# A long convolution and a shift mixer on one core: the filter's transposes in halves by parity, its first DFT step on 64-row tiles, and a new order of work

## The chip, the core and the metric

The kernel runs on one core of a Trainium2 chip. A core has five engines that run side by side, each through its own queue in order: TensorE (PE, matrix products, weights loaded by separate instructions that the profile calls PEld), VectorE (DVE), ScalarE (ACT), GpSimd (POOL) and SyncE (SP), which here issues nearly all DMA transfers. Operands lie in SBUF, 128 partitions wide; PE writes into PSUM, and what PE wrote has to be copied out ("evacuated") by ACT or DVE before the PSUM bank can be used again. The metric is the time of one execution on the device in microseconds; lower is better.

## The reference

Two branches over the same 2048 x 640 input are computed and then mixed by a gate.

```python
g = sigmoid((x * gate_w).sum(-1, keepdims=True))
# A: short causal convolution of k (4 taps), times v, then a long convolution by FFT
k_shift = sum over t<4 of k_pad[:, t:t+S, :] * shift_k[:, 3-t]
kv = k_shift * v
y = irfft(rfft(kv padded to 2S) * rfft(ssm_k padded to 2S))[:S] + kv * ssm_D
a = q * y
# B: a mixer that shifts four channel groups along the sequence, then an MLP
h  = gelu(layernorm(x) @ w1)
hs = concat(shift_1(h0), shift_-1(h1), shift_2(h2), shift_-2(h3)) @ w2
x1 = x + hs
b  = x1 + gelu(layernorm(x1) @ w3) @ w4
return g * a + (1 - g) * b
```

S is 2048, the width D is 640, the MLP's inner width 1536; inputs and output are bf16. `ssm_k` is the filter, given as 640 rows of 2048 time steps.

## The kernel before

The 2048 time steps are laid out as 128 partitions times 16 steps. Branch B is a chain of matmuls with 128-row weights: `mlp1` (w1), `w2`, `w3`, `w4`, with a layer norm before the first and the third. Branch A computes the long convolution as a DFT in steps, all on PE:

- `tap` makes kv from k, v and the four taps, by matmuls with diagonal weights on 64-row tiles.
- `step1` is the first DFT step, of length 128, over the partition axis. It is done for kv (name `KV`) and for the filter (name `HT0`) in four pieces `c` of five units each; a unit is two matmuls, `r` = 0 for the even and 1 for the odd rows, into two PSUM banks. Each bank is evacuated by ACT or DVE, as a string of letters A and V in the step's name says, into a staging buffer `stg`, of which there is one for each `c` and `r`. When all five units are in, `send` stores the buffer to a scratch tensor in DRAM (`S_x` for kv, `S_h` for the filter).
- `gather` reads the scratch back in another order (`ax`); `step2` and its products with `CMP` are the second DFT step, on 64 x 32 tiles; `product` multiplies the two spectra on DVE; `step3` (`INV`) starts the way back on 32 x 64 tiles; its result goes through DRAM again (`S_g`, `gin`), and `step4` (`F4`) finishes, with the gate and q.

The filter has time along the free axis, so `h_transpose` first turns it on PE. In each of ten banks PE transposes eight 128 x 128 blocks whose columns lie 16 elements apart; the block is the stationary operand (the weights), the identity the moving one. The result `HT0` has its rows in natural order. kv has even rows in partitions 0 to 63 and odd ones in 64 to 127, so that its two matmuls of a unit each use half of PE's rows and can run side by side. For the filter the split by parity is in the weights instead: `F1N` is a table of its own with zero rows, and both matmuls use all 128 rows.

Tables of sines are made in the kernel (`f1_table`, `f1n_table`, `f4_table`, `t2_table`, `i_tables`): DVE makes the angles, ACT takes the sine. ACT evaluates sine, GELU and tanh from tables that have to be loaded first, when a function of another table comes up.

The order of all this is written out by hand as one long list, `ORDER`. An entry such as `step1.HT0.2.AAAAAVAAAA:12` names a function, its arguments and the step to issue; the list fixes the order of instructions in each engine's queue. Which buffer of a ring an allocation takes is written out too, in `SLOTS`: "c" for the four PSUM banks, "row" for the four large row buffers that the staging buffers `stg`, the loaded k (`kn`), the normalised x (`xn`) and others share in turn, "gt" and so on. An allocation waits until the last user of its slot is done, a store to DRAM included.

Lines that the profile names and that are spoken of below: L227 warm-up matmuls; L369 and L371 evacuations by ACT and DVE; L395 the filter's transposes; L422 the filter's `step1`, L424 kv's; L434 `send`; L441 `gather`; L462 `step2`; L509 `step3`; L560 and L618 the loads and transposes of k (L618 also x's); L590 `tap`; L709 `mlp1`; L720 the gate's matmuls; L786 `w2`; L813 the transposing DMA of the normalised x1; L834 `w3`; L839 its GELU and L856 `w4`.

Of the kernel before, what the change touches and what calls it, by code (L numbers as in the profile page):

```python
# [16 lines left out]
P = 128  # L17
# [24 lines left out]
def kernel(  # L42
# [24 lines left out]
        "c": "012301230213012310323103120132103123010320130213102321032103230120312013201320132031203102313201"  # L67
             "203213021021323013203210312300123120231203123012130120313021323013223102103120310321032013212032"
             "310230121303120301202130321231030122103032101231302031230123210123012031203103220133012301231023"
             "103120312031201023102",  # L70
        "m": "0100100101010101010101010101010101011010101010110101010101011010101",
        "row": "01230121032130301230123102310320230202023",
        "gt": "012301202120103102012301201",
        "xt": "010101",
        "gq": "012201201102102101202102102101102101",
        "ax": "0123023102130213",
# [32 lines left out]
    F1N = const.tile([P, 2, H, 2], BF16, name="F1N")  # L109
# [53 lines left out]
    def col(i):  # L163
        return sm[:, i:i + 1]
# [87 lines left out]
    def bit(k):  # L252
        return BF[:, k:k + 1]
# [32 lines left out]
    def f1n_table():  # L286

        ts(col(27), bit(0), -1.0, pf[:], op1=ALU.add)
        ts(col(28), col(27), 0.5)
        n = tab([P, H, 2], "n")  # L290
        ts(n[:, :, 0], R64[:, 0:H], col(27), col(28))
        ts(n[:, :, 1], n[:, :, 0], float(128 + 128), op0=ALU.add)
        ts(n[:, :, 0], n[:, :, 0], float(64 + 128), op0=ALU.add)
        yield from sin_table(F1N[:, 0], n, 256)
        yield
        V.tensor_scalar(out=F1N[:, 1], in0=F1N[:, 0], scalar1=bit(0), scalar2=None, op0=ALU.mult)
        V.tensor_tensor(out=F1N[:, 0], in0=F1N[:, 0], in1=F1N[:, 1], op=ALU.subtract)

# [85 lines left out]
    def h_transpose(dc, ev):  # L384
# [4 lines left out]
        def make(hh):  # L389
            box = {}  # L390

            def first():
                ps = box["ps"] = slot(psc, [P, 8, P], BF16, "pst", "c", 4)
                for i in range(8):
                    PE.transpose(out=ps[:, i, :], in_=hv[:, 8 * hh + i, :], identity=IDB[:])  # L395

            def second():
                evac(ev[hh], dst[:, 8 * hh:8 * hh + 8, dc * P:(dc + 1) * P], box["ps"][:])
            return first, second
# [9 lines left out]
    def step1(name, c, ev):  # L409
# [5 lines left out]
        def make(u):  # L415
            ps = []

            def first():
                for r in range(2):
                    ps.append(slot(psc, [P, 512], F32, "ps1", "c", 4))  # L420
                    if name == "HT0":
                        PE.matmul(ps[r][:], lhsT=F1N[:, r].rearrange("p a b -> p (a b)"), rhs=src[:, o + 512 * u:o + 512 * u + 512], start=True, stop=True)  # L422
                    else:
                        PE.matmul(ps[r][:], lhsT=F1[HALF[r]].rearrange("p a b -> p (a b)"), rhs=src[HALF[r], o + 512 * u:o + 512 * u + 512], start=True, stop=True,  # L424
                                  tile_position=(H * r, 0))
# [444 lines left out]
    def step4(t1, ev):  # L870
# [238 lines left out]
```

## Time and profile before

| What | us |
|---|---|
| timed runs, median of 3 (lowest, highest) | 242.7 (242.56, 243.21) |
| the profiled execution | 241.72 |
| its span, first to last instruction | 239.9 |
| PE, DVE, ACT, POOL busy in it | 227.0, 191.6, 176.6, 17.6 |

The profile lists groups of instructions by source line and engine: how often, busy time, mean duration in ns, and then the idle time of the engine just before them with what ended it. A duration is an instruction's own length, and instructions of PE overlap: a matmul of 512 columns is shown with some 380 ns although the next one starts 215 ns later, so PE's pace is read from start to next start. A timeline row gives start, length from the first start to the last end, engine, line, operation, output and input, their shapes, and how many were merged. A row of stretches gives for each engine its busy time and, in brackets, its instruction count, then the granted clock of PE as a share, the DMA engines' share and GB/s.

### The profile page before, as it was taken

To read this page: it belongs to the slowest core of one execution; us is meant where nothing else is said; L and a number is where in the kernel's file an instruction comes from. 1 tells how busy PE (TensorE), PEld (TensorE's weight loads), DVE (VectorE), ACT (ScalarE), POOL (GpSimd) and SP (SyncE) were. 2 spreads that over 40 slices of the span, in tenths; PEclk is the share of its full clock that TensorE was granted. 3 is DMA by queue.
4 is the path that set the end of the run, shared out by engine and by line. 5 is a ranking of instruction groups with operands and counts; after the bars stand their busy time and mean duration, and the time that the engine had idled before them with its cause. 6 is when DMAs were issued, how large, how long until landed. Compare 5 with 4: busy or idle time off the path is not lost.

```text
span 239.9 us, 5658 instructions
## 1 busy us (share of the span) xinstructions
PE 227.0 (95%) x2260; PEld 115.2 (48%) x2260; DVE 191.6 (80%) x454; ACT 176.6 (74%) x318; POOL 17.6 (7%) x34
## 2 busy tenths in 40 slices
PE   6799999999999978889999999999999999999993
PEld 2477575434665534334355344454444455436651
DVE  6999999889889973768769796869768996408994
ACT  4599999779999939998956778848478353636660
POOL 3243220000002000040000300000000000000000
PEclk9999999999999999999999999999999999999998
DMA  6999386793997994998699791089970026599644
GB/s 248 397 369 330 123 188 111 253 351 128 356 401 234 331 271 140 277 380 329 194 304 323 191 245 70 0 158 368 354 221 0 20 93 221 196 378 398 231 164 167
DMA packets 42887, 57.06 MB, mean 238 GB/s; under 512 B 20329, under 2 KB 35690, under 8 KB 42606
## 3 DMA queue, kind: packets, MB, share of 16 engines
q1 hardware_dynamic: 42286, 54.10, 69.7%
q0 software_dynamic: 576, 2.62, 3.1%
q8 instruction: 17, 0.28, 0.5%
q14 instruction: 8, 0.07, 0.1%
HBM read 34.42 MB, written 18.36 MB: 220 GB/s over the span
## 4 chain that ended last, share of the span: by engine, by line
PE 71%; DMA 14%; ACT 8%; DVE 3%; issue 2%; POOL 1%; SPq 0%; ACTq 0%
PE ps L856 18%; PE ps L834 14%; PE psm L709 9%; DMA S_h<-stg 6%; PE psw L786 6%; PE psk L590 4%; PE ps L884 4%; PE ps L462 3%; PE pst L618 3%; PE ps L509 3%; ACT stg L369 3%; DMA ax<-S_h 3%; PE pst L395 2%; PE ps L422 2%; DMA gin<-S_g 2%
## 5 line engine op out<-in xcount | busy, mean ns | idle before, releaser
L856 PE MATMUL ps<-W,gt 128*128 128x512 bf16 (+1 forms) x384 | 56.8, 300 | 0.3 <-ACT gt L839 0.3
L834 PE MATMUL ps<-x1t,W 128*128 128x512 bf16 x240 | 55.6, 380 | 1.0 <-ACT gt L839 1.0
L856 PEld LDWEIGHTS <-gt 128*128 128x128 bf16 x384 | 29.0, 98 | 25.6 <-issue 4.8
L834 PEld LDWEIGHTS <-W 128*128 128x128 bf16 x240 | 21.9, 98 | 30.0 <-issue 6.0
L369 ACT CAST stg<-ps 128x512 bf16<-128x512 f32 x56 | 29.8, 595 | 6.1 <-DMA S_h<-stg 3.8
L369 ACT CAST gs<-ps 128x320 bf16<-128x320 f32 x44 | 16.2, 440 | 18.8 <-PE ps L509 13.6
L839 ACT ACTIVATE gt<-ps 128x1024 bf16<-128x1024 f32 x24 | 24.8, 1041 | 4.1 <-PE ps L834 4.1
L709 PE MATMUL psm<-xt,WA 128*128 128x512 bf16 x100 | 23.6, 380 | 0.0
L371 DVE CAST stg<-ps 128x512 bf16<-128x512 f32 x24 | 15.9, 686 | 7.4 <-PE ps L422 3.6
L786 PE MATMUL psw<-WA,HT 128*128 128x512 bf16 (+1 forms) x116 | 21.7, 299 | 0.0
L369 ACT CAST hs<-ps 128x512 bf16<-128x512 f32 x25 | 13.5, 593 | 8.2 <-PE ps L462 8.2
L371 DVE CAST XS<-ps 128x512 bf16<-128x512 f32 x22 | 14.6, 685 | 4.4 <-PE ps L462 4.4
L888 ACT ACTIVATE y<-ps,GS 128x320 bf16<-128x320 f32 x25 | 12.3, 527 | 7.8 <-PE ps L884 6.1
L786 PEld LDWEIGHTS <-HT 128*128 128x128 bf16 x116 | 10.0, 98 | 11.5 <-issue 2.5
L371 DVE CAST gs<-ps 128x320 bf16<-128x320 f32 x20 | 9.0, 485 | 7.8 <-PE ps L509 5.8
L788 DVE SCALAR_TENSOR_TENSOR X<-psw,X 128x640 bf16<-128x640 f32 x16 | 13.1, 817 | 1.9 <-PE psw L786 1.9
L863 DVE SCALAR_TENSOR_TENSOR X<-ps,OMG,X 128x640 bf16<-128x640 f32 x15 | 13.2, 877 | 1.7 <-PE ps L856 1.7
L709 PEld LDWEIGHTS <-WA 128*128 128x128 bf16 x100 | 9.0, 98 | 11.0 <-issue 1.7
L422 PE MATMUL ps<-HT,F1N 128*128 128x512 bf16 x40 | 11.4, 379 | 2.7 <-ACT stg L369 2.5
L371 DVE CAST hs<-ps 128x512 bf16<-128x512 f32 x15 | 9.9, 685 | 4.1 <-PE ps L462 4.0
L462 PE MATMUL ps<-ax,CMP 64*32 64x384 bf16 (+3 forms) x512 | 13.0, 300 | 0.2 <-DMA ax<-S_h 0.2
L712 ACT ACTIVATE HT<-psm 128x1024 bf16<-128x1024 f32 (+1 forms) x12 | 10.6, 895 | 2.4 <-PE psm L709 2.3
(152 smaller groups left out, 356.2 us busy)
## 6 DMA issues: line engine op xcount, KB each, us to landing
S_x<-stg SPq DMA_DIRECT2D x8, 640.0 KB, 3.0
S_h<-stg SPq DMA_DIRECT2D x8, 640.0 KB, 5.6
ax<-S_x SPq DMA_DIRECT2D x8, 640.0 KB, 5.5
ax<-S_h SPq DMA_DIRECT2D x8, 640.0 KB, 5.9
S_g<-gs SPq DMA_DIRECT2D x8, 640.0 KB, 5.4
W<-in_B_w_dram SPq DMA_DIRECT2D x2, 1920.0 KB, 14.0
kn<-in_A_k_dram SPq DMA_DIRECT2D x4, 640.0 KB, 10.2
q<-in_A_q_dram SPq DMA_DIRECT2D x4, 640.0 KB, 5.7
```

The lines of the kernel that those rows point to most:

```text
L369: A.copy(out=dst, in_=src)
L371: V.tensor_copy(out=dst, in_=src)
L422: PE.matmul(ps[r][:], lhsT=F1N[:, r].rearrange("p a b -> p (a b)"), rhs=src[:, o + 512 * u:o + 512 * u + 512], start=True, stop=True)
L462: PE.matmul(ps[j][q:q + 32, lo - 512 * u:hi - 512 * u], lhsT=CMP[HALF[j], 8 * b + 4 * h + i, c, :], rhs=st[name, 2 * b + h][HALF[j], i, lo ...
L709: PE.matmul(ps[:, v, :].rearrange("p (a b) -> p a b", a=4), lhsT=W1N[:, k, 160 * f:160 * f + P] if f < 4 else W1M[:, k, :], rhs=xt[:, :, k ...
L786: PE.matmul(ps[:, o:o + w], lhsT=h_tile(f, t1), rhs=W2P[:, f, o:o + w], start=(f == 0), stop=(f == 4))
L788: V.scalar_tensor_tensor(out=X1[:, t1, :], in0=ps[:], scalar=1.0, in1=X[:, t1, :], op0=ALU.mult, op1=ALU.add, accum_out=S12[:, 0, t1:t1 + 1])
L834: PE.matmul(ps[:, u, :].rearrange("p (a b) -> p a b", a=4), lhsT=st["W3"][:, k, f * P:(f + 1) * P], rhs=xt[:, :, k, :], start=(k == 0), st ...
L839: A.activation(out=gt[:, 2 * (fp % 2):2 * (fp % 2) + 2, :], in_=ps[:], func=ACT.Gelu_apprx_tanh)
L856: PE.matmul(to[:, 0:w], lhsT=st["gt", c, f // 4][:, f % 4, i * P:(i + 1) * P], rhs=st["W4"][:, f, o:o + w], start=(f == 0), stop=(f == FC ...
L863: V.scalar_tensor_tensor(out=X1[:, t1, :], in0=ps[:], scalar=OMG[:, t1:t1 + 1], in1=X1[:, t1, :], op0=ALU.mult, op1=ALU.add)
L888: A.activation(out=box["y"][:], in_=box["ps"][:], func=ACT.Copy, scale=GS[:, t1:t1 + 1])
```

## The change

Three things change in the code, and with them the order.

`h_transpose` turns each block in two halves: the even columns of the block (one in two, so 32 elements apart in memory) go to PE's column tile 0 and partitions 0 to 63, the odd ones to column tile 64 and partitions 64 to 127. There are 160 transposes of 64 columns for 80 of 128, and `HT0` now has kv's parity order. `step1` for the filter then has the same form as for kv: weights `F1` on half the rows, two 64-row tiles. The table `F1N` and its function are gone. The evacuations, their count and their shapes stay.

`ORDER` and `SLOTS` are written anew. The entries are the same but for the three of `f1n_table`; the letters that give an evacuation to ACT or DVE and the places differ. The diff, cut to the code and to those places of the order that the prediction speaks of:

```diff
-    F1N = const.tile([P, 2, H, 2], BF16, name="F1N")
...
-    def f1n_table():
-
-        ts(col(27), bit(0), -1.0, pf[:], op1=ALU.add)
-        ts(col(28), col(27), 0.5)
-        n = tab([P, H, 2], "n")
-        ts(n[:, :, 0], R64[:, 0:H], col(27), col(28))
-        ts(n[:, :, 1], n[:, :, 0], float(128 + 128), op0=ALU.add)
-        ts(n[:, :, 0], n[:, :, 0], float(64 + 128), op0=ALU.add)
-        yield from sin_table(F1N[:, 0], n, 256)
-        yield
-        V.tensor_scalar(out=F1N[:, 1], in0=F1N[:, 0], scalar1=bit(0), scalar2=None, op0=ALU.mult)
-        V.tensor_tensor(out=F1N[:, 0], in0=F1N[:, 0], in1=F1N[:, 1], op=ALU.subtract)
...
                 for i in range(8):
-                    PE.transpose(out=ps[:, i, :], in_=hv[:, 8 * hh + i, :], identity=IDB[:])
+                    for r in range(2):
+                        PE.transpose(out=ps[HALF[r], i, :], in_=hv[:, 8 * hh + i, r:P:2], identity=IDB[:], tile_position=(0, H * r))
...
-                    if name == "HT0":
-                        PE.matmul(ps[r][:], lhsT=F1N[:, r].rearrange("p a b -> p (a b)"), rhs=src[:, o + 512 * u:o + 512 * u + 512], start=True, stop=True)
-                    else:
-                        PE.matmul(ps[r][:], lhsT=F1[HALF[r]].rearrange("p a b -> p (a b)"), rhs=src[HALF[r], o + 512 * u:o + 512 * u + 512], start=True, stop=True,
-                                  tile_position=(H * r, 0))
+                    PE.matmul(ps[r][:], lhsT=F1[HALF[r]].rearrange("p a b -> p (a b)"), rhs=src[HALF[r], o + 512 * u:o + 512 * u + 512], start=True, stop=True,
+                              tile_position=(H * r, 0))
...
-        "open.L1.left:0 open.A2.right:0 load_x0.0:0 consts0:0 consts0:1 warm:0 load_x0.1:0 load_x.1:0 f1_table:0 warm:1 "
-        "pow0:0 x_stats.0.VVVA:0 f1_table:1 warm:2 kv_alloc:0 x_stats.0.VVVA:1 x_stats.0.VVVA:2 x_stats.0.VVVA:3 "
-        "x_stats.0.VVVA:4 x_stats.0.VVVA:5 x_stats.0.VVVA:6 x_norm.0.AVVA:0 f4_table:0 k_load.3.AAA:0 x_norm.0.AVVA:1 "
+        "open.L1.left:0 open.A2.right:0 consts0:0 load_x0.0:0 warm:0 load_x0.1:0 warm:1 consts0:1 f1_table:0 "
+        "k_load.3.AAA:0 x_stats.0.VVVA:0 x_stats.0.VVVA:1 load_x.1:0 x_stats.0.VVVA:2 pow0:0 kv_alloc:0 warm:2 "
+        "k_load.3.AAA:1 x_stats.0.VVVA:3 x_stats.0.VVVA:4 k_load.3.AAA:5 warm:3 load_w1:0 x_stats.0.VVVA:5 f4_table:0 "
+        "f1_table:1 k_load.3.AAA:6 x_stats.0.VVVA:6 x_norm.0.VVAV:0 warm:4 x_norm.0.VVAV:1 x_norm.0.VVAV:2 "
+        "x_norm.0.VVAV:3 k_load.1.VVA:0 x_stats.1.VVVV:0 k_load.2.VVV:0 x_turn.0.VAA:0 x_turn.0.VAA:4 load_x.3:0 "
...
-        "step1.HT0.1.AVAAVAAVAA:12 x1_norm.0.VVVV:5 w2.11:0 w2.5:1 step1.HT0.1.AVAAVAAVAA:13 step1.HT0.3.AVAAAAAAAA:16 "
-        "w2.11:1 step1.HT0.1.AVAAVAAVAA:9 gate:0 step1.HT0.1.AVAAVAAVAA:11 step1.HT0.1.AVAAVAAVAA:14 "
+        "x1_norm.0.AVAV:4 w2.9:1 t2_table:5 step1.HT0.1.VAAAVAAAAV:12 w2.5:0 x1_norm.0.AVAV:5 w2.11:1 "
+        "step1.HT0.1.VAAAVAAAAV:7 gate:0 step1.HT0.1.VAAAVAAAAV:13 step1.HT0.1.VAAAVAAAAV:9 step1.HT0.3.AAAVAAAAAA:16 "
+        "w2.9:2 w2.5:1 i_tables:2 step1.HT0.1.VAAAVAAAAV:10 w2.6:0 step1.HT0.1.VAAAVAAAAV:14 i_tables:3 "
...
+        "step1.HT0.0.VVVVAVVVAA:6 step1.HT0.0.VVVVAVVVAA:11 w3.0.2:1 w3.0.0:0 step1.HT0.0.VVVVAVVVAA:10 "
+        "step1.HT0.0.VVVVAVVVAA:7 step1.HT0.0.VVVVAVVVAA:3 load_w4:0 w3.0.4:0 gate:1 step1.HT0.0.VVVVAVVVAA:8 w2.4:2 "
+        "step2.x.0.VVVAVAAVVV:12 w3.0.0:1 w3.0.4:1 step1.HT0.1.VAAAVAAAAV:15 step1.HT0.0.VVVVAVVVAA:5 "
```

In the third pair of hunks the buffer in question is the odd-row one of piece 3 (`step1.HT0.3...:16` sends it) and its next user the odd-row one of piece 1, first written by `:11` in the old order and by `:14` in the new one.

More of the change, by code (lines that the diff above doesn't have):

```diff
@@ L66 @@
     SLOTS = {
[L67 to L73, printed above, removed]
+        "c": "012320230213230123203120213203102132030210321301230213021032123021031203102310231203301203120310"
+             "312320132031203132021201303210213203102301202132013032101230123013102130231201321302310312020313"
+             "102130213203102312031023210230101320231213020310231213020312130120312030213310201230123012302130"
+             "213012301230213021031",
+        "m": "0101010101010101010101010101010101010101010101010101010101010101010",
+        "row": "01231023012310012301321302310230021302120",
+        "gt": "01230103130121023102301201",
         "xt": "010101",
-        "gq": "012201201102102101202102102101102101",
-        "ax": "0123023102130213",
+        "gq": "012202120121021021012020120121021021",
+        "ax": "0123021302130213",
         "hp": "01231203",
@@ L902 @@
     ORDER = (
[152 rows of a table removed]
[153 rows of a table added]
     ).split()
     calls = dict(warm=warm, pow0=pow0, row_order=row_order, consts0=consts0, load_w1=load_w1, load_gw=load_gw, w1_mixed=w1_mixed, z_rows=z_rows, z_cols=z_cols, load_x=load_x, load_x0=load_x0, x_norm=x_norm, x_turn=x_turn, x_stats=x_stats,
-                 f1_table=f1_table, f1n_table=f1n_table, t2_table=t2_table, i_tables=i_tables, f4_table=f4_table, kv_alloc=kv_alloc, k_load=k_load, k_wrap=k_wrap, v_load=v_load, tap=tap,
+                 f1_table=f1_table, t2_table=t2_table, i_tables=i_tables, f4_table=f4_table, kv_alloc=kv_alloc, k_load=k_load, k_wrap=k_wrap, v_load=v_load, tap=tap,
                  kv_consts=kv_consts, mlp1=mlp1, load_h=load_h, h_transpose=h_transpose,
```

289 rows, old and new, of the table ORDER are left out of this document.

## The prediction

> **What bounds the kernel now.** I read the page's first part, then busy time by stretches, then the chain that ended last, then TensorE's own timeline.
>
> ```profile
> span 239.9 us, 5658 instructions
> PE 227.0 (95%) x2260; PEld 115.2 (48%) x2260; DVE 191.6 (80%) x454; ACT 176.6 (74%) x318; POOL 17.6 (7%) x34
> ...
> 80.00:90.00 10.00, 8.32 (x53) 4.28 (x52) 8.28 (x23) 5.85 (x13) 0.00 (x0) 1.00 1.10 283
> 90.00:100.00 10.00, 8.96 (x48) 4.11 (x47) 6.28 (x14) 9.94 (x22) 0.00 (x0) 1.00 0.64 206
> 100.00:110.00 10.00, 9.04 (x84) 3.76 (x83) 6.51 (x20) 9.81 (x19) 2.43 (x4) 1.00 1.03 348
> 160.00:180.00 20.00, 20.00 (x264) 8.98 (x262) 16.48 (x26) 12.29 (x24) 0.00 (x0) 1.00 0.92 301
> ```
>
> The columns after a stretch's length are the busy times of PE, PEld, DVE, ACT and POOL. PE is busy for 227.0 of 239.9 us and has no gap at all in a stretch such as 160 to 180. Work taken off PE therefore shortens the kernel, unless something else ends last in that place. The one place in mid-kernel where PE is not full is 80 to 110 us: 1.68 + 1.04 + 0.96 = 3.7 us idle, with ACT full from 90 on. That is the stage of the filter's first DFT step.
>
> ```profile
> PE ps L422 <- ACT stg L369: 2.5, 3, 1.7
> ACT stg L369 <- DMA S_h<-stg: 3.8, 1, 3.8
> ...
> 83.29 5.68 DMA S_h<-stg
> ...
> 105.56 9.35 DMA S_h<-stg
> ...
> 115.88 6.01 DMA ax<-S_h
> 121.94 0.63 PE ps L462 x24
> ```
>
> The waits say why. ACT stood 3.8 us for a staging buffer whose store to DRAM was still on its way (the 5.68 us piece of the chain), and PE then stood for ACT, 1.7 us at the longest. After that the chain runs over ACT and two DRAM trips to the first DFT step 2 of the filter at 121.94.
>
> **The change, part by part.**
>
> *Filter's first step (L422).* Forty full-array matmuls become forty on 64 rows, two of which run side by side. The kernel has that form already, in the same step on KV (L424).
>
> ```profile
> 37.67 0.61 PE L424 MATMUL ps<-KV,F 64*128 64x512 bf16 x4
> 38.21 2.33 PE L709 MATMUL psm<-xt,WA 128*128 128x512 bf16 x10
> ...
> 46.60 0.39 PE L424 MATMUL ps<-KV,F 64*128 64x512 bf16 x2
> 46.83 0.38 PE L590 MATMUL psk<-DG,KT 64*128 64x256 bf16 x4
> ...
> 67.61 0.39 PE L424 MATMUL ps<-KV,F 64*128 64x512 bf16 x2
> 67.93 2.22 PE L395 MATMUL pst<-IDB,HN 128*128 128x128 bf16 x32
> ...
> 71.37 1.03 PE L422 MATMUL ps<-HT,F1N 128*128 128x512 bf16 x4
> 72.23 1.03 PE L786 MATMUL psw<-WA,HT 128*128 128x512 bf16 x4
> ```
>
> From start to next start, four L422 matmuls take 0.86 us; four of L424 take 0.54, two of them 0.32. Two take only 0.23 where another 64-row matmul follows (46.60 to 46.83), so leaving that tiling costs about 0.1 us a visit. In the new order PE visits this step twelve times: eight times with four matmuls, four times with two. New cost 8 x 0.54 + 4 x 0.32 = 5.6 us; old 40 x 0.215 = 8.6. **-3.0 us**, the drains included. No bound is far off here, because the same matmul is in the trace.
>
> *Filter's turn (L395).* Eighty transposes of 128 columns become 160 of 64 columns. The two halves of a pair go to column tiles 0 and 64, each with its own weight load, whose elements now stand 64 bytes apart instead of 32.
>
> ```profile
> 59.12 3.19 PE L395 MATMUL pst<-IDB,E 128*128 128x128 bf16 x48
> 62.15 1.03 PE L786 MATMUL psw<-WA,HT 128*128 128x512 bf16 x4
> ...
> L395 PEld LDWEIGHTS <-E 128*128 128x128 bf16 x48 | 3.1, 148 | 0.3 <-issue 0.3
> L618 PEld LDWEIGHTS <-kn 128*128 128x128 bf16 x80 | 4.9, 96 | 0.5
> L509 PEld LDWEIGHTS <-INV 32*64 32x64 bf16 x256 | 3.0, 102 | 6.5 <-issue 5.0 <-DVE p L483 0.4 <-DVE gs L371 0.4
> L720 PEld LDWEIGHTS <-GW 128*1 128x1 bf16 x20 | 0.4, 82 | 0.6 <-issue 0.2
> ...
> 52.11 1.25 PE L720 MATMUL psz<-xt,GW 128*1 128x512 bf16 x20
> 53.30 0.39 PE L424 MATMUL ps<-KV,F 64*128 64x512 bf16 x2
> ```
>
> Now one costs 3.03/48 = 63 ns, 5.05 us for all eighty. A strided load shows 148 ns against 96 for a packed one, so the load sets that pace. No row shows a half turn, so I bound a pair. Column tiles do run side by side: twenty matmuls in four column tiles took 1.19 us, 0.24 for each four of 512 columns. So the low end is 128 columns at that rate, 0.24/4 = 60 ns, or -0.2 us in all. If a load costs by its columns, two halves cost one whole: 63 ns, 0. If it costs by its length (half of what 148 has over the one-column 82, so 115 ns), a half is 63 x 115/148 = 49 ns, a pair 98, **+2.8**. The high end is two whole prices in a row, 126 ns, +5.05. The trace has a hint for the dear side: the 64-column load of INV, 102 ns, is no shorter than the packed 128-column one, 96. I take the middle of the two readings by columns and by length, 80 ns a pair: **+1.4 us** (-0.2 to +5.1). Two more stretches in a tiling of their own, one of them cut in two, add four drains of 0.1, **+0.4**.
>
> The Trainium skill (SBUF — State Buffer, Specifications) has lines of 16 bytes and a penalty for each new line; elements 32 and 64 bytes apart both open a line each, which by itself would leave the price by columns and the term at 0.
>
> *The stall.* In the old order the buffer that ACT waited for is sent four steps before it is taken again, with two Mixer groups of PE between the matmuls that fill it and those that need it; in the new order six steps and three groups. So part of the wait stays: half of the 1.7 us goes, **-0.9** (0 to -3.7, all that idle time). What is late next there is ACT, full from 90 us.
>
> *Evacuations, table loads, tables.* The filter's forty evacuations (HT0) go from 28 on ACT and 12 on DVE to 27 and 13, KV's from 28 and 12 to 25 and 15.
>
> ```profile
> L369 ACT CAST stg<-ps 128x512 bf16<-128x512 f32 x56 | 29.8, 595 | 6.1 <-DMA S_h<-stg 3.8 <-PE ps L424 1.4 <-PE ps L422 0.7
> L371 DVE CAST stg<-ps 128x512 bf16<-128x512 f32 x24 | 15.9, 686 | 7.4 <-PE ps L422 3.6
> L839 ACT ACT_TABLE_LOAD x2 | 2.6, 1283 | 1.6 <-PE ps L834 1.6
> L273 ACT ACTIVATE F1N<-n,NPI 128x128 bf16<-128x128 int32 x1 | 0.5, 455 | 0.0
> L296 DVE TENSOR_SCALAR F1N<-F1N,BF 128x128 bf16<-128x128 bf16 x1 | 0.3, 256 | 0.0
> ...
> 10.00:20.00 10.00, 9.90 (x107) 7.06 (x108) 9.64 (x31) 9.98 (x16) 4.32 (x6) 1.00 1.01 360
> ```
>
> Four casts move, 4 x 0.6 = 2.4 us off ACT and 2.7 onto DVE, which has 3.7 and 3.5 us free in the two stretches from 90 to 110: no cost, and if that cover is gone at most one cast, 0.7. Sine, GELU, sine, GELU, tanh, GELU is the new succession of tables, six loads for seven: 1.28 us less for ACT late, but tanh now falls between two GELUs of the first w3 groups, two loads where PE needs gt. 0 (-1.3 to +1.3). Without F1N's table ACT saves 0.46 and DVE 0.3, a second pass like it and five small operations. Most of that lies between 10 and 20 us, where PE is full: 0 (-0.5).
>
> *Moved steps.* Twelve of the k transposes go ahead of x's first turn, and their load goes ahead of x's second one in SP's queue.
>
> ```profile
> 1.86 6.57 PE L227 MATMUL psz<-WZ 128*128 128x512 bf16 x20 [1.86 <-DVE WZ L223]
> 10.07 0.62 PE L618 MATMUL pst<-IDB,xn 128*128 128x128 bf16 x8 [1.64 <-ACT xn L661]
> ...
> 15.35 2.01 PE L618 MATMUL pst<-IDB,kn 128*128 128x128 bf16 x32
> 17.20 2.32 PE L709 MATMUL psm<-xt,WA 128*128 128x512 bf16 x10
> ...
> 2.13 0.43 SPq L560 DMA_DIRECT2D kn<-in_A_k_dram  x1
> ...
> L813 SPq DMA_TRANSPOSE x1t<-xn x4: 3024/4141/7513, 85.5 to 156.1; - x4
> ```
>
> They cost 12 x 1.85/32 = 0.7 us of PE and fall into its 1.64 us gap before 10.07, if k is there by then; behind them stand only the last warm matmuls and x's turn, which would wait with them. ACT and DVE are as full as PE right after, so **-0.3** (-0.7 to +0.7, if k comes late). The filter's loads, the load of w3 and the stores and gathers change places in SP's queue by an issue or two, 0.4 us each. The last x1t transpose moves behind four gathers and three S_g stores; SP holds 3 to 7.5 us at each such transpose. Its reader, the last quarter of w3, is far off in PE's order, and PE is full there: 0, up to 4.1 us for one median transpose if that cover is gone. The order from DFT step 2 on has the same visits to each tiling (19 of step 2, 14 of step 3): 0.
>
> Sum: -3.0 + 1.4 + 0.4 - 0.9 - 0.3 = -2.4 us. The profiled execution took 241.7 us (span 239.9 and 1.8 around it), which gives 239.3. The three timed runs have a median of 242.7, 1.0 above it, so I predict **240.3** for the median.
>
> **The rivals.**
>
> *The half loads cost whole ones, one after the other.* Place: PE in the two turn stretches at 59 and 68 us, which have no gap to hide in. Price: a pair 126 ns, +5.05 instead of +1.4; with PE later, no stall is won. -3.0 + 5.05 + 0.4 - 0.3 = +2.1: **244.8**. It decides from a pair of 63 + 2.9/80 us = 99 ns on (111 ns if the stall gain comes). For it: INV's half-width load is as long as a full one. Against it: column tiles overlap in L720, if with one-column loads.
>
> The Trainium skill (TensorEngine Tiling (Array Packing), Restrictions and Gotchas) speaks for this rival: column tiling excludes fast weight load. By another page (TensorE: Matmul & The Clock Gate, LDWEIGHTS), columns over 1.2 give 53 ns a half load; two in a row make 107 a pair, by my estimate +3.5 and a sum of +0.6. INV's row agrees with the first rule.
>
> *PE's gain becomes a wait.* The chain into 121.94 is ACT's evacuations, then 9.35 us of S_h store and 6.01 of gather. If the last store still leaves at 105, PE arrives earlier and waits at step 2 (its wait there is now 0.2 us, so there is no slack): all that is won before is lost, and only the -0.3 at the start may stay: **242.4**. For it: ACT full from 90 to 110. Against: the casts that go to DVE.
>
> *The stage runs without gaps.* Turns at the price by columns (0) and all 3.7 us won: -3.0 + 0.4 - 3.7 - 0.3 = -6.6: **236.1**. For it: DVE is a third idle from 90 to 110 and can take ACT's casts. Against: ACT would have to give up more than four.
>
> **How the numbers follow.** Forecast 0.44, dear half loads 0.23, gain waited away 0.16, no gaps 0.17. Changes under 0.3%, 0.7 us, can't be told from none. Faster: 0.43 of the forecast's, 0.17, and 0.03 of the third; same: 0.01, 0.11 and 0.01 of the dear loads; slower: 0.22 of the dear loads and 0.02 of the third, whose lost cover can cost more than the start gives. So 0.63, 0.13, 0.24. The forecast's own range is 238.3 to 242.0 (turns 0 to +2.8, stall -1.7 to 0). With the two outer cases the range is 236.5 to 245.0: it reaches both of them but for the outer half of each.
>
> **What would show it.** L422's matmuls in fours 0.54 us from start to next start; else the first term is wrong. L395's 160 in 6.4 us: near 5 is the price by columns, near 10 the first rival. The ACT wait for S_h<-stg at two to three us instead of 3.8. The first step 2 of the filter at 119 to 120 instead of 121.94; if it is still there with a PE wait for ax<-S_h of 2 us, the second rival is right. A PE wait in front of x's first turn would mean that k came late.

## The result and the profile after

| What | before | after |
|---|---|---|
| median, us (lowest, highest; 4 runs each) | 242.95 (242.56, 243.23) | 239.88 (239.31, 240.34) |
| the profiled execution and its span | 241.72, 239.9 | 240.33, 238.5 |
| PE busy | 227.0 | 228.1 |
| table loads on ACT (`ACT_TABLE_LOAD`) | 7 | 5 |

The changed kernel takes 0.9874 of the old one's time (95% interval 0.9841 to 0.9906): 3.1 us less, and 0.4 us under the forecast of 240.3. PE's busy time *rose* by 1.1 us; what went is waiting. In the new kernel the filter's turn is L382, the first step L408 (for kv and filter alike), `send` L418, `step2` L446, `step3` L493, evacuations L355 (ACT) and L357 (DVE), `w2` L770, `w3` L818, its GELU L823, `w4` L840, the transposes of k and x L602, `tap` L574, the gate's tanh L807.

The stretches of the stage first, with the columns as before (PE, PEld, DVE, ACT, POOL, clock, DMA, GB/s):

```profile
80.00:90.00 10.00, 10.00 (x72) 4.86 (x70) 9.63 (x28) 9.77 (x21) 1.22 (x2) 1.00 0.85 297
90.00:100.00 10.00, 9.41 (x62) 3.88 (x59) 8.80 (x23) 9.13 (x19) 0.00 (x0) 1.00 1.05 299
100.00:110.00 10.00, 9.91 (x91) 4.04 (x88) 7.39 (x16) 9.16 (x18) 1.11 (x2) 1.00 1.06 385
```

In these stretches PE was idle for 3.7 us before; now it is for 0.7, nearly all of it one wait of 0.59 for the transposed x1. ACT's 3.8 us wait for a sent buffer is gone.

PE's timeline round the filter's turn and first step:

```profile
60.19 1.10 PE L382 MATMUL pst<-IDB,E 128*64 128x128 bf16 x16 [0.49 <-ACT stg L355]
61.23 0.39 PE L408 MATMUL ps<-KV,F 64*128 64x512 bf16 x2
61.55 4.68 PE L382 MATMUL pst<-IDB,E 128*64 128x128 bf16 x80
66.16 1.04 PE L770 MATMUL psw<-WA,HT 128*128 128x512 bf16 x4
...
71.95 3.78 PE L382 MATMUL pst<-IDB,HN 128*64 128x128 bf16 x64
75.67 0.18 PE L720 MATMUL psg<-GW,ones 128*128 128x5 bf16 x1
...
77.16 0.61 PE L408 MATMUL ps<-HT,F 64*128 64x512 bf16 x4
77.70 1.04 PE L770 MATMUL psw<-WA,HT 128*128 128x512 bf16 x4
...
83.18 0.39 PE L408 MATMUL ps<-HT,F 64*128 64x512 bf16 x2
83.50 1.04 PE L770 MATMUL psw<-WA,HT 128*128 128x512 bf16 x4
```

Half turns: 1.04 us for 16, 4.61 for 80, 3.72 for 64, so 9.37 for all 160, 58 to 59 ns each, against 5.08 for the eighty whole ones (59.12 to 62.15, 67.93 to 69.98). First step: fours 0.54, twos 0.32.

The start, and the place where the second DFT step of the filter comes in:

```profile
9.01 0.85 PE L602 MATMUL pst<-IDB,kn 128*128 128x128 bf16 x12 [2.46 <-DMA kn<-in_A_k_dram]
...
11.00 1.28 PE L602 MATMUL pst<-IDB,xn 128*128 128x128 bf16 x20
...
26.67 1.94 PE L574 MATMUL psk<-DG,KT 64*128 64x256 bf16 x44
...
121.99 0.63 PE L446 MATMUL ps<-ax,CMP 64*32 64x512 bf16 x24
...
135.93 0.48 PE L493 MATMUL ps<-hs,INV 32*64 32x320 bf16 x16
136.34 2.33 PE L818 MATMUL ps<-x1t,W 128*128 128x512 bf16 x10
```

k came late, x's first turn begins at 11.00 (10.07 before) and the first taps at 26.67 (25.42). The second step is at 121.99, where it was, with no wait ahead of it: until there PE has won back only what it lost before. `step3` now runs in one piece at 135.93; before, two waits of 0.20 for ACT cut it up, so that its next `w3` began at 137.44 in place of 136.34.

ACT at the first GELUs:

```profile
100.61 1.28 ACT L823 ACT_TABLE_LOAD   x1
101.90 1.02 ACT L823 ACTIVATE gt<-ps 128x1024 bf16<-128x1024 f32 x1
102.82 0.58 ACT L355 CAST stg<-ps 128x512 bf16<-128x512 f32 x1
103.29 0.23 ACT L807 ACTIVATE GS<-ZG 128x16 f32<-128x16 f32 x1
...
104.12 1.02 ACT L823 ACTIVATE gt<-ps 128x1024 bf16<-128x1024 f32 x1
```

The tanh at 103.29 stands between two GELUs and loads nothing.

### The profile page after: what moved, and what is told of

It reads as the page before. It is cut to its first block, busy times and chain, and to the rows that moved or that the text cites. A ratio compares the mean times of both kernels' runs of the same rounds, so it can differ in the third digit from the quotient of the medians.

```text
span 238.5 us, 5806 instructions
## 1 busy us (share of the span) xinstructions
PE 228.1 (96%) x2340; PEld 116.6 (49%) x2340; DVE 191.7 (80%) x443; ACT 176.9 (74%) x318; POOL 16.5 (7%) x34
## 4 chain that ended last, share of the span: by engine, by line
PE 80%; DMA 9%; ACT 7%; issue 1%; DVE 1%; SPq 0%; ACTq 0%
PE ps L840 21%; PE ps L818 18%; PE psm L693 9%; PE psw L770 5%; PE ps L446 5%; PE psk L574 4%; PE pst L382 4%; PE ps L868 4%; PE ps L408 3%; DMA kn<-in_A_k_dram 3%; PE ps L493 3%; DMA x1t<-xn 3%; PE pst L602 3%; ACT stg L355 3%; DMA S_g<-gs 2%; DMA gin<-S_g 2%
## 5 line engine op out<-in xcount | busy, mean ns | idle before, releaser
L840 PE MATMUL ps<-W,gt 128*128 128x512 bf16 (+1 forms) x384 | 56.8, 300 | 0.3 <-ACT gt L823 0.3
L818 PE MATMUL ps<-x1t,W 128*128 128x512 bf16 x240 | 55.6, 380 | 0.7 <-DMA x1t<-xn 0.6
L840 PEld LDWEIGHTS <-gt 128*128 128x128 bf16 x384 | 28.9, 98 | 25.3 <-issue 4.7
L818 PEld LDWEIGHTS <-W 128*128 128x128 bf16 x240 | 21.8, 98 | 29.7 <-issue 5.4
L355 ACT CAST stg<-ps 128x512 bf16<-128x512 f32 x52 | 28.2, 604 | 7.2 <-PE ps L408 6.2
L355 ACT CAST gs<-ps 128x320 bf16<-128x320 f32 x44 | 16.2, 435 | 17.5 <-PE ps L493 16.6
L823 ACT ACTIVATE gt<-ps 128x1024 bf16<-128x1024 f32 x24 | 24.7, 1034 | 4.4 <-PE ps L818 4.4
L770 PE MATMUL psw<-WA,HT 128*128 128x512 bf16 (+1 forms) x116 | 21.7, 300 | 0.0
L357 DVE CAST XS<-ps 128x512 bf16<-128x512 f32 x24 | 15.7, 685 | 7.3 <-PE ps L446 7.2
L357 DVE CAST stg<-ps 128x512 bf16<-128x512 f32 x28 | 18.7, 686 | 2.9 <-PE ps L408 1.9
L355 ACT CAST hs<-ps 128x512 bf16<-128x512 f32 x27 | 14.5, 592 | 7.0 <-PE ps L446 7.0
L770 PEld LDWEIGHTS <-HT 128*128 128x128 bf16 x116 | 9.2, 98 | 11.5 <-issue 4.6
L357 DVE CAST gs<-ps 128x320 bf16<-128x320 f32 x20 | 9.4, 486 | 5.6 <-PE ps L493 5.5
L446 PE MATMUL ps<-ax,CMP 64*32 64x512 bf16 (+3 forms) x512 | 12.9, 299 | 0.0
L775 ACT ACTIVATE jk<-X 128x640 bf16<-128x640 bf16 x16 | 12.0, 749 | 0.0
L471 DVE TENSOR_TENSOR XS<-XS,hs 128x2560 bf16<-128x2560 bf16 x8 | 11.9, 1485 | 0.1
L770 PE MATMUL psw<-WA,HM 128*128 128x512 bf16 (+1 forms) x44 | 11.8, 299 | 0.0
```

The lines of the kernel that those rows point to most:

```text
L355: A.copy(out=dst, in_=src)
L357: V.tensor_copy(out=dst, in_=src)
L446: PE.matmul(ps[j][q:q + 32, lo - 512 * u:hi - 512 * u], lhsT=CMP[HALF[j], 8 * b + 4 * h + i, c, :], rhs=st[name, 2 * b + h][HALF[j], i, lo ...
L770: PE.matmul(ps[:, o:o + w], lhsT=h_tile(f, t1), rhs=W2P[:, f, o:o + w], start=(f == 0), stop=(f == 4))
L775: A.activation(out=jk[:], in_=X1[:, t1, :], func=ACT.Square, accum_out=S12[:, 1, t1:t1 + 1])
L818: PE.matmul(ps[:, u, :].rearrange("p (a b) -> p a b", a=4), lhsT=st["W3"][:, k, f * P:(f + 1) * P], rhs=xt[:, :, k, :], start=(k == 0), st ...
```

## The experiments

Each ratio is to the kernel of before on the same chip; on it a microsecond is 0.0041. In most cuts of `ORDER` below, entries stand one to a line; where an edit moves or drops an allocation, its entry in `SLOTS` goes with it.

### Code and order apart

The kernel has two parts that come apart: the new code and the new order. First the new code with the old `ORDER` and `SLOTS`:

```diff
-        "open.L1.left:0 open.A2.right:0 consts0:0 load_x0.0:0 warm:0 load_x0.1:0 warm:1 consts0:1 f1_table:0 "
+        "open.L1.left:0 open.A2.right:0 load_x0.0:0 consts0:0 consts0:1 warm:0 load_x0.1:0 load_x.1:0 f1_table:0 "
...
```

> The changed transposes and the changed first step, in the order and slots of before (without the three entries of the F1N table). Theory (the order brings the gain, the code costs): the half turns show 58 ns each, 9.3 us in all against 5.1, and four more drains; they lie in stretches in which PE is full, while only about half of the 3.0 us from the 64-row step lies where PE sets the pace (before 82 us); the ACT wait for S_h<-stg stays near 3.8 us. 244 to 245.5 us, slower than before. Rival (the code brings the gain, whatever the order): 240 to 241 us, and faster than before.

Measured: 245.27 us, ratio 1.0117 (1.0091 to 1.0143), slower than before by some 2.8 us. The dear turns took part of ACT's wait for a sent buffer with them: 2.4 us, where it was expected to stay near 3.8. Then the old code, `F1N` and whole turns, with the new order (the three steps of `f1n_table` put in at the places where they were among their neighbours):

```diff
         x_turn.0.VAA:3
+        f1n_table:0
...
+        f1n_table:1
         mlp1.0.0:1
...
+        f1n_table:2
         step1.KV.2.AVAAVVVAVA:9
```

> The whole-block transposes, F1N and 128-row first step of before, in the order and slots of after (three entries for the F1N table put back). Theory (order): the turns take 5.1 us again and the first step 8.6, a net of 4.2 + 0.4 - 3.0 = 1.6 us less for PE than after; no ACT wait for S_h<-stg over 1 us, six table loads; 238.0 to 239.0 us, faster than the changed kernel. Rival (code): without the 64-row step the gain is gone, 242 us or more.

Measured: 238.25 us, ratio 0.9806 (0.9790 to 0.9823), which beats both kernels (with five table loads, as in the changed kernel, not the six expected). So the order alone is worth -4.7 us, and the code costs: +2.8 in the old order (2.2 to 3.5), 0.9874 - 0.9806 = 0.0068 or +1.6 us in the new one (0.8 to 2.5, if the two intervals are taken as independent). The two prices differ, but their intervals overlap. The change is faster in spite of what it computes differently.

### The start

In the changed kernel k's first transposes wait 2.46 us for their load, and x's turn waits behind them. Here they stand behind x's turn:

```diff
-        k_load.3.AAA:1
...
-        k_load.3.AAA:5
...
-        k_load.3.AAA:6
...
         x_turn.0.VAA:3
+        k_load.3.AAA:1
+        k_load.3.AAA:5
+        k_load.3.AAA:6
```

> The changed kernel with the twelve early k transposes and their one early evacuation put back behind x's first turn, its k load left where it is. Theory (k came late and x's turn waited behind it): the PE wait of 2.5 us for kn goes, x's first turn starts at 10.0 to 10.3 us instead of 11.0, and the first taps at 26.0 or before instead of 26.67; 239.0 to 239.6 us, 0.3 to 0.9 less than the changed kernel. Rival (ACT and DVE set the pace up to 50 us, the PE wait costs nothing): the first taps at 26.6 us as before the edit, 239.9 us.

Measured: 239.92 us, ratio 0.9879 (0.9860 to 0.9897), no gain. x's turn began at 9.76, yet the first taps came at 27.66, later still. This profile alone can't say why: after PE's 2.12 us of waiting in front of x's turn, the clock granted to it was 0.73 from 10 to 12 us and 0.50 from 12 to 14. The old code in the new order had the full clock there and no wait for k, and its first taps came at 27.73: PE waited for DVE's evacuations instead (1.02 and 1.46 us). Then that kernel (old code, new order) with the old order's 108 entries up to the first tap in front, and the rest behind them as it was:

```diff
-        open.L1.left:0 open.A2.right:0 consts0:0 load_x0.0:0 warm:0 load_x0.1:0 warm:1 consts0:1 f1_table:0
+        open.L1.left:0 open.A2.right:0 load_x0.0:0 consts0:0 consts0:1 warm:0 load_x0.1:0 load_x.1:0 f1_table:0
...
```

> The kernel of before with the changed kernel's order, as in the run with the old code, except that all steps up to the first tap of k stand in before's order. Theory (the new start is worse: first taps at 27.7 us there against 25.4, since DVE is late with x's turn): first taps near 25.4 and 236.0 to 237.2 us. Rival (the start's delay is swallowed by the wait for v, for the square sums or the loads further on): 237.8 to 238.6 us.

Measured: 238.16 us, ratio 0.9811 (0.9785 to 0.9836), no change from 0.9806; the rival held. Its taps came at 27.27, not at 25.4, and that is the finding:

```profile
22.44 1.08 PE L618 MATMUL pst<-IDB,kn 128*128 128x128 bf16 x16 [0.64 <-DVE xt L371]
23.77 0.62 PE L618 MATMUL pst<-IDB,kn 128*128 128x128 bf16 x8 [0.24 <-DVE xt L371]
...
27.27 1.94 PE L590 MATMUL psk<-DG,KT 64*128 64x256 bf16 x44 [0.72 <-ACT KT L369]
```

The first two of these waits are also in three other profiles with the old start (the old order with the new code, and the two runs below that change the kernel of before further on; first taps at 26.57, 26.59 and 26.44 us), and only the profile of before has none. The new start varies too: 26.67 us in the changed kernel, but 24.72 in the run below with a step of 4 bytes, on another chip, where the wait for k was 0.20 us. So the 1.25 us between the two profiles lies within what one and the same start differs by, and by the ratios the two starts can't be told apart. That a late start is free is not shown: from the first taps to the filter's first turn it is 33.3 to 33.7 us in every profile but that of POOL's copies, so the delay is still there at 60 us.

### The stall

The kernel of before; three of the staging rows of the filter's first step are put into columns of KV, which is dead by then:

```diff
-        "row": "01230121032130301230123102310320230202023",
+        "row": "01230121032130301230122310320230202023",
...
-                    stg[r] = slot(ring, [P, 4 * D], BF16, "stg", "row", ROW)
+                    b = (2 * (1 - c) + r - 1) if name == "HT0" and c < 2 else -1
+                    stg[r] = st["KV"][:, 4 * b * D:4 * b * D + 4 * D] if b >= 0 else slot(ring, [P, 4 * D], BF16, "stg", "row", ROW)
```

> The kernel of before, all of its code and order, but three of the eight staging rows of the filter's first step (both halves of block 0, the second half of block 1) are written to the columns of KV, which is dead by then, so that none of them waits until a row already sent has landed. Theory (the stall is worth what the tensor engine idles there: 25 - 21.3 = 3.7 us in 80 to 105, of which the wait for the sent row is most): 239.0 to 240.5 us, no wait of ACT for S_h<-stg, tensor engine idle in 80 to 105 under 1.5 us. Rival (the prediction's price: another wait takes three quarters of it, -0.9): 241.5 to 242.3 us.

Measured: 239.17 us, ratio 0.9839 (0.9820 to 0.9858), -3.9 us (-4.4 to -3.5) with ACT's wait for a sent buffer gone. Its stretches of the stage:

```profile
80.00:90.00 10.00, 10.00 (x66) 5.30 (x65) 9.70 (x25) 9.62 (x20) 0.00 (x0) 1.00 1.09 295
90.00:100.00 10.00, 9.28 (x52) 4.43 (x50) 6.97 (x16) 9.91 (x20) 0.00 (x0) 1.00 1.02 297
100.00:110.00 10.00, 10.00 (x117) 4.18 (x117) 7.48 (x22) 9.42 (x17) 2.43 (x4) 1.00 1.06 395
```

PE's idle time falls from 3.7 to 0.7 us, as in the changed kernel. PE's waits of 1.68, 0.56 and 0.26 us for the staging buffers are gone. ACT is as full as before from 90 on, yet PE waits for it only once, 0.72 us for a GELU at 99.94 (0.96 before). So no other wait in this stage took the place of this one. 3.0 of the 3.9 us are PE's idle time here; where the rest lies was not traced.

### The table loads

The kernel of before; the sine of the last inverse table goes ahead of the first GELU, the tanh behind it:

```diff
-        "gt": "012301202120103102012301201",
+        "gt": "012301202120100312012301201",
...
         w3.0.2:0
-        gate:1
...
+        i_tables:5
+        i_tables:6
         w3.0.2:1
...
         w3.0.4:0
-        i_tables:5
...
         w3.0.4:1
+        gate:1
...
         scale_x1.5.V:0
-        i_tables:6
```

> The kernel of before; alone the last sine of the inverse table and the gate's tanh change places with the first GELUs (the sine goes ahead of them, the tanh behind), so that ACT loads one table in place of four from 90 us on. Theory (the load at 133.2 and the order of ACT's work around it held the first piece of step 3 up, 1.1 us): 241.2 to 242.0 us. Rival (ACT is not what the end waits for, the prediction's price of nothing): 242.3 to 243.1 us.

Measured: 242.04 us, ratio 0.9955 (0.9936 to 0.9974), -1.1 us (-1.6 to -0.6), 0.04 us past the theory's span. From 90 us on ACT loads one table, at 100.42, and `step3` runs in one piece at 137.15. Stall and tables together make -5.0 us; the whole order made -4.7 (-5.1 to -4.3). If the two add up (no run has both), they account for it.

### The price of a half turn

What makes a half turn as dear as a whole one? The first try was the kernel of before with the filter turned in halves by place, not by parity (columns 32 bytes apart, as in a whole turn), and one piece of k, whose columns are neighbours, turned in halves too:

```diff
-                    PE.transpose(out=ps[:, i, :], in_=hv[:, 8 * hh + i, :], identity=IDB[:])
+                    for r in range(2):
+                        PE.transpose(out=ps[HALF[r], i, :], in_=hv[:, 8 * hh + i, HALF[r]], identity=IDB[:], tile_position=(0, H * r))
```

> The kernel of before with each of the filter's transposes in two halves on two column tiles, but in natural order (columns 0 to 63 and 64 to 127, elements 32 bytes apart as in whole blocks), and the twenty transposes of k's piece 1 in halves of packed columns. Theory A (a column tile's weight load costs what a whole block's does, whatever the stride): filter halves at about 58 ns from start to next start, loads of about 200 ns; packed halves at 50 ns or more. Theory B (the wider stride doubled the price of an element): filter halves at about 32 ns, 64 a pair, and packed halves at 28 or so, 56 a pair.

```profile
15.62 1.36 PE L621 MATMUL pst<-IDB,kn 128*64 128x128 bf16 x40
16.92 0.87 PE L625 MATMUL pst<-IDB,kn 128*128 128x128 bf16 x12
...
L396 PEld LDWEIGHTS <-E 128*64 128x64 bf16 x96 | 5.9, 217 | 0.3 <-issue 0.3
L621 PEld LDWEIGHTS <-kn 128*64 128x64 bf16 x40 | 1.2, 109 | 0.4 <-issue 0.4
```

k's forty halves took 1.30 us, 32 ns each, and a load of theirs 109 ns; the filter's 61 ns each, with 217. Each theory was half right: it isn't the tile, and it isn't the step of 64 bytes over 32; it is that there is a wide step at all. (The run took 253.1 us, of which some 4 to 5 were lost in the start, first taps at 30.82: PE waited 2.23 us for an evacuation by DVE, and its granted clock was 0.57 from 24 to 28 us. So its total says nothing of the turns.) Next the changed kernel with neighbouring columns, and then with smaller steps (`hv` is the row of 2048 times; the filter is shuffled in all three):

```diff
-        hv = st.pop(("HN", dc)).rearrange("p (q t1) -> p t1 q", t1=NT)
+        hv = st.pop(("HN", dc)).rearrange("p (t1 q) -> p t1 q", t1=NT)
...
-                        PE.transpose(out=ps[HALF[r], i, :], in_=hv[:, 8 * hh + i, r:P:2], identity=IDB[:], tile_position=(0, H * r))
+                        PE.transpose(out=ps[HALF[r], i, :], in_=hv[:, 8 * hh + i, HALF[r]], identity=IDB[:], tile_position=(0, H * r))
```

The step of 4 bytes keeps the old second line (`r:P:2`) behind the new first one; for 8 and 16 bytes the second line takes `hv[:, o:o + H * q - q + 1:q]`, with q 8 for E and 4 for HN.

> The changed kernel; the filter's half turns take 64 neighbouring times of a row as the stationary operand in place of every 32nd (the times come out in another order, so the convolution is of a shuffled filter; instructions, shapes, waits and transfers are the same). Theory (a half's price is the stride of its weight load): weight loads near 110 ns, a half at 30 ns, 160 x 30 = 4.8 us in place of 9.3, and the time at 235.0 to 236.3 us. Rival 1 (the halves wait on their evacuations once they are cheap): halves at 30 ns within a bank, but 237.5 to 239.3 us. Rival 2 (a half is dear here for another reason, the tile's place or the output): halves still at 55 ns or more, 239.3 to 240.5 us.

> As the run with neighbouring columns, but a half takes every second time of 128 neighbouring ones (a step of 4 bytes between the columns; again a shuffled filter). Theory (any step between columns costs, however short): loads near 200 ns and a half at 55 to 60 ns as with 64 bytes. Rival (only steps beyond a line of several neighbours cost): loads near 110 ns and 30 ns a half, or something between, 40 ns, in the proportion of the bytes passed over.

> As the run with a step of 4 bytes, but in the 96 half turns from E the 64 columns lie 16 bytes apart, and in the 64 from HN 8 bytes (again a shuffled filter). 4 bytes took 110 ns a load and 30 ns a half, 32 and 64 bytes 204 to 217 ns and 58 to 61. Theory (what counts is how many 16-byte pieces of a row the columns touch: 8 of them at 2 bytes, 16 at 4, and the double price once each column lies in a piece of its own): HN still at 110 ns and 30, or little above, E at 204 and 58. Rival (the price grows with the step): HN near 140 ns and 40, E near 170 and 50. Rival 2 (the limit lies beyond 16 bytes): both at 110 and 30.

Measured: 236.39 us, ratio 0.9719 (0.9696 to 0.9742) with neighbours, 0.09 us past the theory's span; one run each of the others, 234.67 and 236.72 us beside 241.8 and 241.4 for the kernel of before on their chips. The groups of weight loads (busy, mean ns): of the changed kernel, columns 64 bytes apart,

```profile
L382 PEld LDWEIGHTS <-E 128*64 128x64 bf16 x96 | 5.7, 204 | 1.0 <-issue 1.0
```

with neighbouring columns (the row for 4 bytes reads the same),

```profile
L382 PEld LDWEIGHTS <-E 128*64 128x64 bf16 x96 | 2.9, 110 | 1.1 <-issue 1.1
```

and 16 bytes apart in E, 8 in HN:

```profile
L383 PEld LDWEIGHTS <-E 128*64 128x64 bf16 x96 | 6.0, 213 | 1.0 <-issue 1.0
L383 PEld LDWEIGHTS <-HN 128*64 128x64 bf16 x64 | 2.0, 144 | 0.2 <-issue 0.2
```

| step between 64 columns, bytes | 2 | 4 | 8 | 16 | 32 | 64 |
|---|---|---|---|---|---|---|
| pieces of 16 bytes touched | 8 | 16 | 32 | 64 | 64 | 64 |
| a weight load, ns | 110 | 110 | 144 | 213 | 217 | 204 |
| a half turn, start to start, ns | 30 | 30 | 33 | 61 | 61 | 58 |

A half's price is read from the timelines: 80 of them from 60.79 to 63.23 us with neighbours, with 4 bytes the same length (2.51 us, to the last end), with 16 bytes a length of 4.95 us; 64 with 8 bytes from 70.14 to 72.23. (Where E and HN have one step, their loads are alike: 204 and 204, 110 and 110.) For 4 bytes the theory failed and the rival held. For 8 and 16 bytes the theory had the paces, though the load of 144 ns is what the rival expected. The price is nearly flat up to 32 pieces and doubles at 64, where it stays at steps of 16, 32 and 64 bytes. All six columns fit 0.92 ns for each 16-byte piece (59/64), but no less than 30 ns, to within 4 ns; a limit on the step itself, between 8 and 16 bytes, would fit them as well. The forecast's guess by columns and the one by the length of a load both miss this. With 30 ns a half the changed kernel wins 4.5 us of PE, and 0.9874 - 0.9719 = 0.0155, 3.8 us, reach the end.

### A packed filter with its true times

If a half is cheap on neighbouring columns, an idle engine can put them side by side. POOL does it, block by block:

```diff
+        hn = st["HN", dc].rearrange("p (q r t1) -> p t1 r q", r=2, t1=NT)
...
+                G.tensor_copy(out=x[:, a - o:b - o, r, :], in_=hn[:, a:b, r, :])
...
-                        PE.transpose(out=ps[HALF[r], i, :], in_=hv[:, 8 * hh + i, r:P:2], identity=IDB[:], tile_position=(0, H * r))
+                        PE.transpose(out=ps[HALF[r], i, :], in_=hv[8 * hh + i][:, r, :], identity=IDB[:], tile_position=(0, H * r))
```

> The changed kernel, with its true times again: POOL, which idles there, copies each block of the filter (128 x 2048) into another place with the even times of a group before the odd ones, so that a half turn's 64 columns are neighbours, and the half turns read the copy; everything else is as in the changed kernel, but the load of W3 now waits for the turn of block 3 too. Theory (a half costs 30 ns on neighbouring columns, and the copies hide behind 25 us of idle POOL): 235.2 to 237.0 us, halves at 30 ns. Rival 1 (POOL's strided copies last longer than 4 us a block, and the turns wait for them): a wait of the tensor engine for POOL and 238.5 to 245 us. Rival 2 (POOL's copies slow DVE's or ACT's work of the same time, or the later W3 costs as much): halves at 30 ns but 237.5 to 239.5 us.

Measured: 245.91 us, ratio 1.0169 (1.0141 to 1.0198). The halves cost 30 ns, and the kernel is slower than before. DVE's timeline at the beginning of POOL's copies (34.8 to 44.2 us):

```profile
34.74 0.41 DVE L601 TENSOR_TENSOR KV<-yk,KV 128x512 bf16<-128x512 bf16 x1
35.08 0.68 DVE L604 TENSOR_TENSOR KV<-psk,KV 128x512 bf16<-128x512 f32 x1
35.68 1.67 DVE L663 TENSOR_SCALAR xn<-X,RS,NB 128x640 bf16<-128x640 bf16 x2
...
39.76 1.26 DVE L601 TENSOR_TENSOR KV<-yk,KV 128x512 bf16<-128x512 bf16 x1
```

and PE's, with the stretch behind it:

```profile
45.28 0.38 PE L590 MATMUL psk<-DG,KT 64*128 64x256 bf16 x3 [4.14 <-DVE stg L373]
```

```profile
46.00:50.00 4.00, 4.00 (x22) 1.12 (x17) 2.42 (x6) 1.66 (x4) 0.00 (x0) 0.57 0.07 24
```

The product of two SBUF operands takes 1.26 us in place of 0.41, the normalised x 1.67 in place of 0.79 for two; an operation with one operand in PSUM keeps its 0.68. PE then waits 4.14 us for DVE, and the clock granted to it in 46 to 50 is 0.57, so that it is busy and slow. The second rival named this contention, but put the time at 239.5 us at most; it is 6.4 more. The wait for POOL itself, the first rival's, is 1.3 us (0.55 and 0.75, in the turn of block 4). PE shows no wait for W3. An estimate from these rows: PE's waits for DVE in this stage and the next (4.14 and 2.07), for POOL (1.3) and the slow clock (4.00 x 0.43 = 1.7) make 9.2 us, of the 10.9 by which this kernel is above the one with neighbouring columns (1.0169 - 0.9719).

## Why the prediction was right, and where it was not

The number was right by luck: two of its terms were off by 3 us each, in opposite directions. By its terms the code was to bring -1.2 us (-3.0 + 1.4 + 0.4) and the order -1.2 (-0.9 - 0.3); the runs give +1.6 and -4.7.

| term | predicted | found |
|---|---|---|
| filter's first step | -3.0 | -3.0 (0.54 and 0.32, its own numbers) |
| half turns | +1.4 | 9.37 - 5.08 = +4.3 |
| two more stretches in a tiling | +0.4 | not told apart |
| stall | -0.9 | -3.9 (removed alone) |
| table loads, evacuations, F1N's table | 0 | -1.1 (loads moved alone) |
| twelve k transposes moved | -0.3 | none to be seen |
| sum | -2.4 | -3.7; measured -3.1 (-3.9 to -2.3) |

**Half turns.** The step that failed is the bound chosen: "the middle of the two readings by columns and by length", 80 ns a pair. It measured 117, near the 126 of the first rival, which had the price right. The readings by columns and by length stood on loads of neighbouring columns or of one column, and half of what the strided load of 148 ns has over a one-column one was taken to go with the columns. The half's load shows 204, longer than the whole one's. The Trainium skill (SBUF — State Buffer, Specifications) has lines of 16 bytes and a penalty for each new one. The steps of 2 to 64 bytes agree with it. The prediction had this rule and drew the wrong sum from it: 32 and 64 bytes do cost the same, but a whole strided turn of 128 lines takes 63 ns and a half with 64 lines takes 58, so the price by columns didn't follow. Why a whole-array load takes twice as many lines in its time no run here tells. By the Trainium skill (TensorEngine Tiling (Array Packing), Restrictions and Gotchas) a column tile goes without fast weight load, which would fit, but no run here turns that on or off. The 53 ns a load that the prediction worked out by the Trainium skill (TensorE: Matmul & The Clock Gate, LDWEIGHTS) don't settle it either: packed halves come every 30 ns, 60 on each of the two tiles, which would fit if the tiles load side by side, and then the strided ones, 117 a tile, are dearer than that.

**The stall.** "So part of the wait stays: half of the 1.7 us goes" took PE's longest single wait for the whole price, and named ACT as late next. The wait went altogether, and the run with the spare rows shows that 3.0 of PE's 3.7 us idle time hung on it: three waits for staging buffers went with it, and the later one for the GELU became shorter. The first rival's remark that "with PE later, no stall is won" failed, and with it the rival: dear turns did come, and the stall was won as well. It was right in part: in the old order the dear turns alone brought ACT's wait from 3.8 to 2.4 us. The third rival had this term right, and the turns wrong.

**Tables.** The "two loads where PE needs gt" did not come; once GELU's table is in, tanh needs none (103.29). There are 5 loads for 7, and the one at 133.21 is gone, behind which the casts stood that `step3` waited for. This was worth 1.1 us, inside the bounds given (-1.3 to +1.3) but not at the value taken.

**The start.** k came late, as the upper bound allowed, and PE waited for it as named. It cost nothing that the medians can show: with the k transposes behind x's turn, and with the whole old start, the kernels took as long. PE's waits for DVE's evacuations vary from profile to profile by as much; what a late start costs by itself stays open.

**The marks.** L422's successor has its fours at 0.54. The turns are near 10 us, not 6.4: the sign given for the first rival. ACT's wait for S_h<-stg is 0, not two to three us. The filter's second step stands at 121.99, not at 119 to 120, but with no wait ahead of it: the second rival, a wait at `step2`, did not come. PE was simply no earlier there, since the 4.3 of the turns and the later start of this profile had used up nearly all that step and stall gave.

## What to carry to other kernels

A change of code that comes with a new order should be taken apart into both before it is credited: here the code costs 1.6 us and the order brings 4.7, and the old code in the new order is the best kernel of the study that leaves the filter unshuffled (0.9806; with the old start 0.9811). A wait of the engine that evacuates was worth here at least what TensorE idled in the whole stage behind it, not its longest single wait there. And cutting a stationary operand in two made each part cheaper only where its columns lay close: packed, a half took 30 ns and a whole 58; with a step of 32 bytes a half took 61 and a whole 63.

## What was not expected of the hardware

- A weight load of 64 columns on a column tile and its transpose cost 30 to 33 ns up to 32 pieces of 16 bytes touched, and about 60 at 64 pieces, the same for steps of 16, 32 and 64 bytes; nothing in between was run. Two packed halves (60 ns) cost what a whole packed turn of k does (32 from 15.35 to 17.20 in the kernel before, 58 ns).
- POOL's strided copies (1.05 to 1.14 us for 128 x 512 bf16) stretch DVE's operations on SBUF operands to two and three times their length (0.79 to 1.67 us, 0.41 to 1.26), and leave those that read PSUM alone (0.68). The Trainium skill (SBUF — State Buffer, SBUF: two separate sides) has DVE and GpSimd share one pair of ports under an exclusive lock; the rows agree.
- Profiles of one and the same start differ by over 1 us in when the first taps begin (25.42 to 26.59 in the old code and order), more than the 0.7 us below which the forecast counted a change as none. A single pair of profiles could not have told the start's price.
- The clock granted to PE fell behind a stretch with little PE work in three profiles (0.57 behind the 4.14 us wait, 0.57 behind 2.9 us idle from 20 to 24, 0.50 behind 2.12), but not behind the changed kernel's 2.46 us wait for k. When it falls the runs here don't tell.
